# Router logits of seven blocks: VectorE products with a running sum in place of TensorE transposes and matmuls

## Chip, cores and metric

One core of one Trainium2 chip. The metric is the device time of one execution in microseconds (us); lower is better. Engines are called by the names of the profile: PE is TensorE (PEld its weight loads), DVE is VectorE, ACT is ScalarE, POOL is GpSimd, SP is SyncE, which here only issues DMAs.

## The reference, cut to what matters

```python
# attention over keys and values pooled by 8, 8 heads of 64, 8 batches of 576 rows
x = attention(q, k, v)                      # 4608 rows of 512
h = x @ w_in                                # 4608 x 2048
g = where(h >= 1, h, where(h <= -1, 0, (h + 1)**2 / 4))
x = g @ w_out                               # 4608 x 512, called Y below
logits = x @ w_gate                         # 4608 x 8
e = argmax(logits); p = softmax(logits)[e]
out = p * (relu(x @ w1[e]) @ w2[e])         # each row with the weights of its own expert
```

The change concerns the line `logits = x @ w_gate` alone.

## The kernel before

The 4608 rows are 36 tiles of 128 rows, grouped in ten blocks: block 0 has 3 tiles, blocks 1 to 7 have 4, block 8 has 3 and block 9 has 2. A block is one pass over `w_in` and `w_out` in 16 steps, called m = 0 to 15 here. Step m of block j issues, in this order: `f1` for two steps ahead (12 matmuls with the hidden rows as output), slot 2m, `f2` for step m (3 matmuls for each tile, summed in one PSUM bank per tile over the 16 steps), slot 2m+1. Each engine runs its own queue in the order in which the code emits it, so this order is the order on PE, DVE, ACT, POOL and SP.

Behind each `f1` stands a chain over two engines: DVE cuts to -1..1 (line 489, here the clip), ACT squares (490), DVE takes the maximum (494), ACT rounds to the high part (495), DVE writes the low part (501, here the last link). `f1` of step m uses the PSUM bank of step m-2, so it can only start when the last link of step m-2 is done; `f2` of a step needs the same link of its own step. The maximum is emitted in slot 2m and the last link in slot 2m+1.

A slot also takes units of the attention of the next block from a list (`units`): transposes and small matmuls on PE, softmax work on DVE, ACT and POOL, and the pooling of keys and values on DVE (line 212). Units and routing share two PSUM banks in turn. Last, a slot takes steps of the routing of the block before from a queue, `todo`: one step in even slots and two in odd ones, and two in every slot of blocks 8 and 9. Empty steps stand in the queue for spacing.

`route_steps(j)` fills that queue for block j at the start of block j+1. For each tile, `turn` transposes the rows of Y on PE (4 transposes) and ACT copies the result to `YT`. `logits_t` multiplies with the gate weights `WGT` (4 matmuls of 512 columns, seen as 8 in the trace), ACT copies to `LT`. `logits` transposes back (one per tile) and DVE adds up into `LG` (line 550). Then `s1` picks the expert (DVE lines 563 to 569), `s2` finds the position of each row (DVE lines 579 to 590) and SP stores Y to `yrow_d` (line 591), and `s3` has POOL scatter the row numbers with one indirect DMA per tile (line 598). `YT` and `LT` lie in the tile `WG`, which is otherwise free in these blocks. SP issues the loads of the first expert's weights (line 667) after the store of block 7's rows.

Of the kernel before, what the change touches and what calls it, by code (L numbers as in the profile page):

```python
# [8 lines left out]
F32 = mybir.dt.float32  # L9
# [3 lines left out]
ACTF = mybir.ActivationFunctionType  # L13
ALU = mybir.AluOpType
# [9 lines left out]
def attention_ffn_routed_experts_kernel(  # L24
# [12 lines left out]
    nc = tc.nc  # L37
    B, H, S, D = q.shape
    NT, DM = out.shape
    DFF = w_in.shape[1]  # L40
    NE, _, EF = w1.shape
    NTILE = NT // 128
    SP_ = S // 8
    KD = DM // 128
# [12 lines left out]
    blocks, t = [], 0  # L57
# [3 lines left out]
    NB = len(blocks)  # L61
# [5 lines left out]
    dram = ctx.enter_context(tc.tile_pool(name="dram", bufs=1, space=bass.MemoryType.DRAM))  # L67

    wo_d = dram.tile([KF, 128, 2, DM], F32R, name="wo_d")
    yrow_d = dram.tile([NT + 128, ROW], F32, name="yrow_d")  # L70
    perm_d = dram.tile([NE * CAP, 1], I32, name="perm_d")

# [13 lines left out]
    FX = sb.tile([128, 4112], F32, name="FX")  # L86
    Y = sb.tile([128, 4, ROW], F32, name="Y")
    WG = sb.tile([128, NE, DM], F32, name="WG")
    YO = [WG[:, 4 + i] for i in range(4)]
    YT = WG[:, 0:4]  # L90
    LT = WG[:, 4]
    WGT = sb.tile([128, KD, NE], F32, name="WGT")
# [4 lines left out]
    def fx(o, n):  # L97
# [11 lines left out]
          for a in [YF[:, 0:1024], YF[:, 1024:2048], at(5312, 1024)]  # L109
          + [WG.rearrange("p e d -> p (e d)")[:, 1024 * i:1024 * (i + 1)] for i in range(3)]]  # L110
    JK = at(6848, 512)
# [17 lines left out]
    ident = sb.tile([128, 128], F32, name="ident")  # L129
# [31 lines left out]
    LG = sb.tile([128, 4, NE], F32, name="LG")  # L161
# [59 lines left out]
    def bank():  # L221
        banks.rotate(-1)
        return banks[-1]
# [29 lines left out]
    SCH = at(6848, 576)  # L253
    WGF = WG.rearrange("p e d -> p (e d)")[0:SP_]
    PTX = [WOF[2][0:SP_], WOF[3][0:SP_]] + [WGF[:, 3072 + 512 * i:3584 + 512 * i] for i in range(2)]
# [191 lines left out]
    n = FIRST  # L447
# [74 lines left out]
    def route_steps(j, bk):  # L522
        t0, n = blocks[j]
# [3 lines left out]
        V = nc.vector  # L527
        st = []

        def turn(t):  # L530
            pb = bk()
            for c in range(KD):
                nc.tensor.transpose(pb[:, c * 128:(c + 1) * 128], Y[:, t, c * 128:(c + 1) * 128],
                                    ident)
            nc.scalar.activation(out=YT[:, t], in_=pb, func=ACTF.Copy)

        def logits_t():

            pb = bk()
            for c in range(KD):  # L540
                nc.tensor.matmul(pb[32 * c:32 * c + NE, 0:n * 128], WGT[:, c],
                                 YT[:, 0:n, c * 128:(c + 1) * 128], start=True, stop=True)
            nc.scalar.activation(out=LT[:, 0:n * 128], in_=pb[:, 0:n * 128], func=ACTF.Copy)
# [7 lines left out]
                out=lg, in_=pb[:, 0:n * 128].rearrange("p (t c x) -> p t x c", c=KD, x=32)[:, :, 0:NE],  # L551
                axis=AX.X, op=ALU.add)

        wait = 2 if j < NB - 2 else 1
        for t in range(n):
            st.append(lambda t=t: turn(t))
            st.extend([lambda: None] * wait)
        for f in (logits_t, logits):
            st.append(f)
            st.extend([lambda: None] * wait)  # L560

        def s1():
            V.tensor_reduce(out=mx, in_=lg, axis=AX.X, op=ALU.max)
# [365 lines left out]
    with tc.manual_schedule():  # L929

        pre = [WG[0:SP_, i] for i in range(8)]
        raw0 = pre + RAW + [FX[0:SP_, 512 * i:512 * (i + 1)] for i in range(1, 5)] + [JK[0:SP_]]
# [100 lines left out]
        for g, (j, m) in enumerate(steps):  # L1033
            if m == 0:
                if j:
                    evict_y(j - 1)
                    todo.extend(route_steps(j - 1, bank))
                    banks.clear()
                    banks.extend(ps[6:8])
                lim = blocks[j + 1][0] + blocks[j + 1][1] - 1 if j + 1 < NB else -1  # L1040
                cnt = 0
                for i, u in enumerate(units):
                    if u[0] <= lim:
                        cnt = i + 1
                state["units"], state["done"] = cnt, 0
                if j == 1:

                    nc.vector.memset(JK, 0.0)
                    nc.vector.memset(Y[:, :, DM:ROW], 0.0)
                    nc.scalar.dma_start(out=yrow_d[NT:NT + 128, 0:DM], in_=JK)  # L1050
                    nc.scalar.dma_start(out=yrow_d[NT:NT + 128, DM:ROW], in_=Y[:, 3, DM:ROW])
            if g + AHEAD < len(steps):
                f1(*steps[g + AHEAD])
            else:
                f1e(0, g + AHEAD - len(steps))
            slot(j, 2 * m)
            f2(j, m)
            if (j, m) == (0, KF - 2):
                more_consts()
                nc.vector.memset(CB[:, 0], 0.0)  # L1060

                pr = at(6848, NE * CAP // 128).bitcast(I32)
                nc.gpsimd.iota(pr, pattern=[[1, NE * CAP // 128]], base=0,
                               channel_multiplier=NE * CAP // 128)
                nc.vector.tensor_scalar(pr, pr, 127, None, op0=ALU.bitwise_and)
                nc.vector.tensor_scalar(pr, pr, float(NT), None, op0=ALU.add)
                nc.sync.dma_start(out=perm_d.rearrange("(p r) o -> p (r o)", p=128), in_=pr)
            slot(j, 2 * m + 1)
        evict_y(NB - 1)
        todo.extend(route_steps(NB - 1, bank))  # L1070
# [166 lines left out]
```

## Time and profile before

| what | us |
|---|---|
| median of 3 runs (1577.69 to 1592.39) | 1578.44 |
| profiled execution | 1580.64 |
| its span, first to last instruction | 1578.9 |
| PE busy | 1457.9 (92%) |
| DVE busy | 793.5 (50%) |
| ACT busy | 489.0 (31%) |
| POOL busy | 214.0 (14%) |

The blocks can be told by line 519, the copies of Y at a block's end: block 1 begins at 191.9 us, block 2 at 299.9, 3 at 408.6, 4 at 517.2, 5 at 625.7, 6 at 734.1, 7 at 843.3, 8 at 944.9, 9 at 1030.2; the expert part begins at 1105.0. Matmuls overlap in the records: one of 512 columns is shown with 0.39 us and the next starts 0.23 us later, so PE's cost is read from start to start. The same holds for DVE: an instruction that waits for nothing starts before the record of the one ahead has ended.

### The profile page before, as it was taken

What the parts mean: (1) busy time and instruction counts of PE and PEld (TensorE: products, weight loads), DVE (VectorE), ACT (ScalarE), POOL (GpSimd) and SP (SyncE); (2) the same over time, 40 slices, a digit from 0 to 9 for tenths busy, and PEclk for the clock granted to TensorE, in tenths of its full rate; (3) what the DMA queues carried; (4) which work ended last, traced back from release to release, by engine and by line L of the source; (5) the groups of instructions that cost most, each with busy time, mean ns of one, the idle gap of its engine ahead of it and who ended that gap; (6) DMA issues with size and microseconds to landing.
All of it is one profiled execution on the core that took longest, in us unless ns stands there. A gap on an engine that the chain in (4) does not pass through costs nothing. (4 is left out here: it accounts for less than half of the span.)

```text
span 1578.9 us, 19781 instructions
## 1 busy us (share of the span) xinstructions
PE 1457.9 (92%) x7415; PEld 1185.9 (75%) x7415; DVE 793.5 (50%) x1547; ACT 489.0 (31%) x900; POOL 214.0 (14%) x216
## 2 busy tenths in 40 slices
PE   5677799999999999999999999886699999999797
PEld 4566677778777777777778788775588888888685
DVE  6898756646555654665654445343232222212425
ACT  5344332333332333332333333232111111111334
POOL 4222101001001001001010010002321111111211
PEclk8899999999999999999999999997899999999999
DMA  8566436427629456465475384974141101110403
GB/s 226 161 207 198 134 118 122 127 90 126 131 90 142 122 109 97 130 128 95 132 105 97 100 89 137 201 155 86 41 168 54 54 28 40 44 51 28 159 28 140
DMA packets 102550, 177.28 MB, mean 112 GB/s; under 512 B 46594, under 2 KB 54933, under 8 KB 102432
## 3 DMA queue, kind: packets, MB, share of 16 engines
q10 hardware_dynamic: 21552, 75.79, 24.0%
q1 hardware_dynamic: 73392, 79.93, 17.8%
q0 software_dynamic: 7488, 20.07, 4.3%
q8 instruction: 64, 1.05, 0.3%
q14 instruction: 54, 0.44, 0.1%
HBM read 171.05 MB, written 28.29 MB: 126 GB/s over the span
## 5 line engine op out<-in xcount | busy, mean ns | idle before, releaser
L482 PE MATMUL ps<-XT,W 128*128 128x512 f32 (+2 forms) x640 | 252.1, 394 | 9.1 <-DVE FG L501 8.4
L510 PE MATMUL ps<-WO,FG 128*128 128x512 f32 x576 | 241.6, 419 | 20.2 <-ACT WO L438 10.7
L483 PE MATMUL ps<-XT,W 128*128 128x512 f32 (+2 forms) x640 | 239.9, 375 | 3.0 <-DVE XT L344 3.0
L484 PE MATMUL ps<-XT,W 128*128 128x512 f32 (+2 forms) x640 | 240.0, 375 | 1.5 <-POOL W L226 1.5
L511 PE MATMUL ps<-WO,FG 128*128 128x512 f32 x576 | 230.7, 400 | 3.9 <-POOL WO L226 2.7
L490 ACT ACTIVATE FX<-FX,half 128x512 f32<-128x512 f32 (+2 forms) x152 | 104.0, 684 | 413.7 <-DVE FX L489 406.7
L512 PE MATMUL ps<-WO,FG 128*128 128x512 f32 x576 | 229.9, 399 | 0.0
L489 DVE TENSOR_SCALAR FX<-ps 128x512 f32<-128x512 f32 (+2 forms) x152 | 96.6, 635 | 181.8 <-PE ps L484 181.6
L820 DVE SCALAR_TENSOR_TENSOR FG<-ps,FG 128x512 fp32r<-128x512 f32 (+1 forms) x64 | 43.2, 675 | 220.7 <-ACT FG L819 220.7
L510 PEld LDWEIGHTS ps<-WO,FG 128*128 128x128 f32 x576 | 110.5, 192 | 51.2 <-issue 13.5
L482 PEld LDWEIGHTS ps<-XT,W 128*128 128x128 f32 x640 | 123.5, 193 | 32.0 <-DVE FG L501 9.7
L484 PEld LDWEIGHTS ps<-XT,W 128*128 128x128 f32 x640 | 123.0, 192 | 21.7 <-POOL W L226 2.4
L483 PEld LDWEIGHTS ps<-XT,W 128*128 128x128 f32 x640 | 123.7, 193 | 19.9 <-DVE XT L344 3.9
L495 ACT ACTIVATE FG<-ps 128x512 fp32r<-128x512 f32 (+2 forms) x160 | 88.9, 555 | 148.1 <-DVE ps L494 136.7
L511 PEld LDWEIGHTS ps<-WO,FG 128*128 128x128 f32 x576 | 111.0, 193 | 26.4 <-POOL WO L226 4.1
L512 PEld LDWEIGHTS ps<-WO,FG 128*128 128x128 f32 x576 | 110.6, 192 | 25.1
L494 DVE TENSOR_TENSOR ps<-FX,ps 128x512 f32<-128x512 f32 (+2 forms) x152 | 97.4, 640 | 56.6 <-ACT FX L490 56.6
L501 DVE TENSOR_TENSOR FG<-ps,FG 128x512 fp32r<-128x512 f32 (+2 forms) x160 | 100.8, 630 | 39.7 <-ACT FG L495 39.7
L819 ACT ACTIVATE FG<-ps 128x512 fp32r<-128x512 f32 (+1 forms) x64 | 37.5, 585 | 266.0 <-PE ps L816 265.5
L317 POOL TENSOR_TENSOR AT<-AT,ssm 128x576 f32<-128x576 f32 x36 | 42.6, 1186 | 488.6 <-DVE ssm L310 422.3
L814 PE MATMUL ps<-XT,W 128*128 128x512 f32 (+1 forms) x256 | 99.0, 387 | 0.0
L815 PE MATMUL ps<-XT,W 128*128 128x512 f32 (+1 forms) x256 | 98.6, 385 | 0.0
(215 smaller groups left out, 2281.1 us busy)
## 6 DMA issues: line engine op xcount, KB each, us to landing
WO<-wo_d ACTq DMA_DIRECT2D x144, 512.0 KB
AT<-in_moe_w_dram SPq DMA_DIRECT2D x10, 2048.0 KB
AT<-in_moe_w_dram SPq DMA_DIRECT2D x14, 1024.0 KB
AT<-in_v_dram SPq DMA_DIRECT2D x60, 144.0 KB
AT<-in_q_dram SPq DMA_DIRECT2D x32, 256.0 KB
wo_d<-WO SPq DMA_DIRECT2D x16, 512.0 KB
AT<-in_k_dram SPq DMA_DIRECT2D x56, 144.0 KB
yrow_d<-Y SPq DMA_DIRECT2D x7, 1032.0 KB
```

The source lines that it names most:

```text
L482: nc.tensor.matmul(o, wi(m, 0, c), xh, start=(c == 0), stop=False)
L483: nc.tensor.matmul(o, wi(m, 0, c), xl, start=False, stop=False)
L484: nc.tensor.matmul(o, wi(m, 1, c), xh, start=False, stop=(c == KD - 1))
L489: nc.vector.tensor_scalar(r, o, -1.0, 1.0, op0=ALU.max, op1=ALU.min)
L490: nc.scalar.activation(out=r, in_=r, func=ACTF.Square, scale=0.5, bias=half)
L494: nc.vector.tensor_tensor(out=o, in0=r, in1=o, op=ALU.max)
L501: nc.vector.tensor_tensor(out=gl, in0=o, in1=r32(gh), op=ALU.subtract)
L510: nc.tensor.matmul(o, gh, WO[:, g % 4, 0], start=(m == 0), stop=False)
L511: nc.tensor.matmul(o, gh, WO[:, g % 4, 1], start=False, stop=False)
L512: nc.tensor.matmul(o, gl, WO[:, g % 4, 0], start=False, stop=(m == KF - 1))
L814: nc.tensor.matmul(o, e1(0)[:, c, ms], xh, start=(c == 0), stop=False)
L815: nc.tensor.matmul(o, e1(0)[:, c, ms], xl, start=False, stop=False)
```

## The change

For blocks 1 to 7 the steps `turn`, `logits_t` and `logits` are gone. In their place stand 32 instructions `logit(t, e)` on DVE, one for each tile and expert: 512 products of a row of Y and a gate column, with their sum in `LG`. They come in pairs, one pair to a step of the queue. For blocks 1 to 6 an empty step follows most pairs, so that a tile takes 7 steps of the queue; for block 7 there is none, and a slot of block 8 takes two pairs. The products themselves go to the scratch `JK`, the same one each time. The gate columns must lie along the row on every partition: at the start of block 1, PE transposes `WGT` (4 transposes), ACT copies, SP stores 16 KB to DRAM (`wg_d`), and at step 13 of block 1 ACT's queue issues a DMA that loads it to all 128 partitions of `WG` (2 MB). Blocks 0, 8 and 9 keep the way of before.

```diff
+        def logit(t, e):
+            V.scalar_tensor_tensor(out=JK, in0=Y[:, t, 0:DM], scalar=1.0, in1=WG[:, e],
+                                   op0=ALU.mult, op1=ALU.mult, accum_out=LG[:, t, e:e + 1])
...
-        wait = 2 if j < NB - 2 else 1
-        for t in range(n):
-            st.append(lambda t=t: turn(t))
-            st.extend([lambda: None] * wait)
-        for f in (logits_t, logits):
-            st.append(f)
-            st.extend([lambda: None] * wait)
+        if 0 < j < NB - 2:
+            for i in range(0, n * NE, 2):
+                st.append(lambda i=i: [logit(*divmod(x, NE)) for x in (i, i + 1)])
+                st.extend([lambda: None] * (j < NB - 3 and i % 8 > 0))
+        else:
+            wait = 2 if j < NB - 2 else 1
+            for t in range(n):
+                st.append(lambda t=t: turn(t))
+                st.extend([lambda: None] * wait)
+            for f in (logits_t, logits):
+                st.append(f)
+                st.extend([lambda: None] * wait)
...
+                    pb = bank()
+                    for c in range(KD):
+                        nc.tensor.transpose(pb[0:NE, c * 128:(c + 1) * 128], WGT[:, c], ident)
+                    nc.scalar.activation(out=LT[0:NE], in_=pb[0:NE], func=ACTF.Copy)
+                    nc.sync.dma_start(out=wg_d, in_=LT[0:NE])
...
+            if (j, m) == (1, 13):
+                nc.scalar.dma_start(out=WG, in_=wg_d.unsqueeze(0).to_broadcast([128, NE, DM]))
```

## Rows read from the trace of the kernel before

**Rows 1.** Windows by block (1, 3): length, busy us of engines, PEclk, DMA share, GB/s.

```profile
191.90:299.90 108.00, 105.52 (x553) 83.85 (x552) 70.26 (x128) 36.50 (x68) 7.76 (x7) 1.00 0.54 128
...
408.60:517.20 108.60, 107.72 (x565) 85.89 (x564) 65.42 (x122) 36.93 (x68) 8.49 (x8) 1.00 0.58 122
```

**Rows 2.** Timeline of PE in block 3: start, us, instruction, idle before and releaser.

```profile
413.06 0.63 PE L533 MATMUL ps<-ident,Y 128*128 128x128 f32 x4 [0.88 <-DVE AT L300]
...
420.22 0.66 PE L533 MATMUL ps<-ident,Y 128*128 128x128 f32 x4
420.63 0.47 PE L510 MATMUL ps<-WO,FG 128*128 128x512 f32 x1
...
441.06 1.04 PE L541 MATMUL ps<-WG,WGT 128*8 128x512 f32 x8
442.04 0.50 PE L510 MATMUL ps<-WO,FG 128*128 128x512 f32 x1
```

**Rows 3.** Windows of steps m=0 to 8 (blocks 3, 2, 5, 7), then m=0 to 3 of block 8.

```profile
411.30:475.95 64.65, 63.77 (x348) 50.54 (x347) 39.52 (x83) 23.01 (x42) 4.46 (x4) 1.00 0.36 115
...
302.58:367.61 65.03, 64.16 (x360) 50.30 (x359) 33.16 (x75) 22.41 (x40) 4.46 (x4) 1.00 0.29 90
...
628.35:693.15 64.80, 63.92 (x348) 50.73 (x347) 45.87 (x90) 23.22 (x42) 4.45 (x4) 1.00 0.42 129
...
845.96:906.82 60.86, 60.86 (x336) 48.69 (x335) 28.14 (x65) 20.39 (x36) 3.30 (x3) 1.00 0.28 93
947.36:969.40 22.04, 22.04 (x134) 18.94 (x133) 11.39 (x33) 8.49 (x16) 1.14 (x1) 1.00 0.36 129
```

**Rows 4.** DVE instructions with two SBUF inputs: a line's durations (ns), a group's mean.

```profile
L427 DVE SCALAR_TENSOR_TENSOR FX<-AT,FX x5: 672/682/685, 38.3 to 149.7; 128x512 int32<-128x512 int32 x5
...
L891 DVE TENSOR_TENSOR W<-AT,W 128x1024 fp32r<-128x1024 f32 x14 | 16.5, 1222 | 11.8 <-ACT W L889 6.1 <-ACT FX L863 5.7
```

**Rows 5.** Timeline of DVE in block 3.

```profile
409.37 1.28 DVE L517 COPY Y<-ps 128x512 f32<-128x512 f32 x2
...
472.57 0.18 DVE L581 TENSOR_TENSOR G<-ps,CB 128x32 f32<-128x32 f32 x1
472.79 0.17 DVE L583 COPY CB<-CB 128x8 f32<-128x8 f32 x1
472.87 0.19 DVE L584 TENSOR_TENSOR G<-G,ebase 128x32 f32<-128x32 f32 x1
```

**Rows 6.** Timeline of ACT in the first tile's softmax, with a sum as second output.

```profile
23.67 0.32 ACT L296 ACTIVATE AT<-ps,smx 128x72 f32<-128x72 f32 x1 [2.91 <-PE ps L283]
23.89 0.19 ACT L296 ACTIVATION_READ_ACCUMULATOR AT<-ps,smx 128x1 f32 x1
23.98 0.31 ACT L296 ACTIVATE AT<-ps,smx 128x72 f32<-128x72 f32 x1
```

**Rows 7.** Timeline of POOL and DVE in block 0.

```profile
45.31 1.74 POOL L226 TENSOR_TENSOR W<-FX,W 128x512 fp32r<-128x512 f32 x1 [3.63 <-ACT W L438]
...
45.93 1.66 DVE L427 SCALAR_TENSOR_TENSOR FX<-WG,FX 128x512 int32<-128x512 int32 x1
```

**Rows 8.** Waits of DVE from 411.30 to 475.95 us: total, times, longest.

```profile
DVE XT L344 <- ACT XT L343: 5.2, 5, 1.1
...
DVE ps L494 <- ACT FX L490: 2.4, 3, 0.8
```

**Rows 9.** Timeline of block 3: the last link of a step, and the `f1` that waits for it.

```profile
418.90 0.68 DVE L501 TENSOR_TENSOR FG<-ps,FG 128x512 fp32r<-128x512 f32 x1
...
423.82 0.48 PE L482 MATMUL ps<-XT,W 128*128 128x512 f32 x1
```

**Rows 10.** Block 8: SP's loads of expert weights, then PE's longest wait (timelines).

```profile
984.57 2.78 SPq L667 DMA_DIRECT2D AT<-in_moe_w_dram  x4
...
1007.60 0.76 PE L510 MATMUL ps<-WO,FG 128*128 128x512 f32 x1 [5.15 <-DMA WO<-wo_d]
```

**Rows 11.** The page's DMA queues, ACT's: packets, MB, share of 16 engines.

```profile
q10 hardware_dynamic: 21552, 75.79, 24.0%
```

More of the change, by code (lines that the diff above doesn't have):

```diff
@@ L69, in attention_ffn_routed_experts_kernel @@
     wo_d = dram.tile([KF, 128, 2, DM], F32R, name="wo_d")
+    wg_d = dram.tile([NE, DM], F32, name="wg_d")
     yrow_d = dram.tile([NT + 128, ROW], F32, name="yrow_d")
```

## The prediction

> **What bounds the kernel now.** I read the windows cut at the block boundaries first. In block 3 PE is busy for 107.7 of 108.6 us at the full granted clock and DVE for 65.4 [rows 1]. So PE sets the length of these blocks, and what is taken off PE shortens them, as long as the other queues keep up. Block 1 shows where that ends: there DVE has 70.3 us of work in 108.0, and PE already loses 2.5 us [rows 1]. Then I read PE's timeline for the price of the routing steps, the windows of the steps m = 0 to 8, in which the new DVE work is to stand, and last DVE's waits and the slack between its last link and the `f1` that needs it.
>
> **What goes off PE.** A turn takes 0.41 us from its start to the next matmul's, `logits_t` 0.98 [rows 2], and I take 0.41 again for the four transposes back: 4 x 0.41 + 0.98 + 0.41 = 3.0 us a block. The first turn also waits 0.88 us for a bank that DVE still reads [rows 2]; the same wait stands once in each of blocks 2 to 6. That makes 3.9 us in these five and 3.0 in blocks 7 and 8, 25.5 us in all. This is the ceiling of the gain. ACT's five copies a block go too; ACT is idle most of the time, so I price them at nothing.
>
> **What one logit costs DVE.** No row shows a DVE product with a running sum, so I bound it. The main instruction has two SBUF inputs of 512 four-byte elements, as line 427 has: 0.68 us [rows 4]. Two copies that wait for nothing take 1.28 us together, so the second starts 0.60 us after the first [rows 5]. On ACT the sum comes out by an instruction of its own, which starts 0.22 us after a main one of 0.32 us and holds the queue for 0.09 us more [rows 6]. Lower end: 0.60 for the main one and 0.08 for a small one that waits for nothing (L583 to L584 [rows 5]), 0.68 us. Upper end: both run to their end, with 0.04 us each before the next starts: 0.68 + 0.04 + 0.17 + 0.04 = 0.93 us. I take 0.80: the read overlaps as on ACT (0.60 + 0.17), but the next product overwrites the same `JK`, and L583, which overwrites what L581 reads, starts 0.22 us after it, which is its 0.18 and 0.04 more [rows 5]. That adds 0.04. So 32 logits are 25.6 us a block, between 21.8 and 29.8.
>
> The Trainium skill ("VectorE: DVE Perf Modes", section "Two Vector instructions with no wait between them") also has an accumulator output as two instructions; no row here shows that for DVE, and if the read were free the sum would be that of the lower end.
>
> **Whether DVE keeps up.** The steps of `todo` put the 32 logits into m = 0 to 8 (28 steps of the queue at 1.5 a slot), and s1 and s2, which stood there, move behind. These are some 20 small instructions with the sum of line 550, at 0.2 us each (0.18 and 0.04 [rows 5]): 4.0 us less. In its order DVE also has idle time that no later work can fill: it waits for ACT within its own chains, 5.2 + 2.4 = 7.6 us in these nine steps [rows 8]. So for m = 0 to 8 of block 3 DVE needs 39.5 - 4.0 + 25.6 + 7.6 = 68.7 us, and PE, 3.9 us lighter, 64.65 - 3.9 = 60.8 [rows 3]. DVE becomes the bound, by 7.9 us. Part of it is slack: the last link ends at 419.58 and the `f1` that needs it starts at 423.82 [rows 9], 4.2 us later. PE then waits 7.9 - 4.2 = 3.7 us, and of the 3.9 us 0.2 are left. Block 4 has the same work. Block 2, from its own row: 33.2 - 4.0 + 25.6 + 7.6 = 62.4 against 61.1, inside the slack: gain 3.9. Block 7: 28.1 - 4.0 + 25.6 + 7.6 = 57.3 against 57.9: gain 3.0 [rows 3]. Blocks 5 and 6 have more pooling in these steps [rows 3]: 45.9 - 4.0 + 25.6 = 67.5 if the pooling fills the waits, 75.1 if not, against 60.9. After the slack PE waits 2.4 to 10.0 us; I take the middle, 6.2, a loss of 2.3 each. Blocks 2 to 7 together: 3.9 + 0.2 + 0.2 - 2.3 - 2.3 + 3.0, a gain of 2.7 us. The logits stand behind the maximum and the last link in DVE's queue, so it is the next clip, softmax pieces and the low part of attention rows that come late, and through them `f1` and the units two banks on.
>
> **Block 8** is where it hurts. Two pairs stand in each slot, so all 32 logits lie in m = 0 to 3, which last 22.0 us and have 11.4 us of DVE work [rows 3]. DVE needs 11.4 + 25.6 and for four steps 0.85 us of waits each (7.6 / 9), 40.4 us; PE 22.0 - 3.0 = 19.0. After 4.2 us of slack PE waits some 17 us, a loss of 14. Some comes back: later in the block PE waits 5.15 us for a load of `w_out` that shares the DMA engines with the expert weights [rows 10]. These loads stand behind Y's store on SP and so behind s2, which is now one slot earlier in order but late by DVE's lag. If PE arrives later than the loads do, the wait shrinks, by 0 to 5.15; I take 2.5. Loss of block 8: 11.5 us.
>
> **The rest.** The prelude of block 1 is one turn more on PE, 0.5 us. The 2 MB to all partitions: ACT's queue moves 75.79 MB in 24% of the span of 16 engines [rows 11], 379 us, so 2.1 MB are some 10.5 us; it is issued near 288 us (step 13 of block 1) and first needed after the maximum of block 2's first step, near 305. The cover is 17 us, and I price it at nothing; if it lands late, the first logit holds the whole DVE queue, at most 10 us once. `w_out` loads queue behind it on ACT's ring, but each is issued three steps, some 20 us, before its use. On SP one store of 16 KB more is nothing; SP's loads of queries and keys pass the later s2 in order, so nothing of theirs waits for it longer. Y's store moves from m = 8 to m = 11 and needs to land by the block's end, some 25 us later: hidden. POOL: a two-input DVE instruction took 1.66 us beside a POOL instruction of 1.74 [rows 7], 1.0 more than alone. POOL's softmax product runs 4 times a block; if two in five meet a logit in the steps that DVE bounds, that is 2 us.
>
> **Sum.** -2.7 + 11.5 + 0.5 + 2.0 = +11.3 us. Against the profiled execution, 1580.6, that is 1591.9; the median of the runs lies 2.2 us lower, so 1589.7, and I say 1589. A measurement of this kernel can tell about 1% (16 us), so this is no change that can be told, leaning to slower.
>
> **Rivals.** (1) DVE has room and the ceiling is paid out: 65.4 us of its 108.6 are used, 19 or 25 more still fit on average. Then the time is 1578.4 - 25.5 + 0.5 = 1553. It holds if the logits fall into DVE's waits for PE rather than beside work. Against it: the order is fixed, the logits fill nine steps of sixteen, and block 1 loses time at 70 us. 14%. (1b) The cheap end, 0.68 us: 3.8 us less a block. Blocks 3 and 4 then gain 3.9 each, blocks 5 and 6 1.5, block 8 loses 7.7: -17.7 + 7.7 + 0.5 + 1 = -8.5, 1570; within 1%. 13%.
> (2) Slower: the read of the sum does not overlap, 0.93 us a logit. It decides from about 0.83 on, where the sum passes 1%. Then blocks 3 to 6 and 8 lose 4.2 us more each and block 2 leaves its slack by 1.3: 11.3 + 21.0 + 5.2 = 37.5 at most, 1612 to 1616. 22%.
> (3) The product with a sum runs at half rate. Line 427 has two four-byte SBUF inputs and is not halved [rows 4], but it writes no sum. At half rate the main one costs what 1024 elements do, 1.22 us [rows 4], with 0.13 for the read 1.35; that is 0.55 x 32 = 17.6 us a block more in five blocks, 14.7 in block 2 and 12.8 in block 7: +127, 1705. 8%.
> The Trainium skill ("Vector Engine (DVE) Microarchitecture Reference", section "Points that are easy to get wrong") says so: this shape with two SBUF sources that are not bf16 halves throughput, as no read port is left for the accumulator. By that rule the time is that of rival 3; the trace speaks neither for nor against it where a sum is written.
>
> **How the numbers follow.** My forecast (0.72 to 0.88 us a logit) has 43%, and three quarters of it lie within 1%, the rest above. With 1b: same 0.44; slower 0.40 (rivals 2, 3 and that rest); faster 0.16 (rival 1 and a little of 1b). The range of 8 in 10 goes from near rival 1 to beyond rival 2, 1556 to 1624; rival 3 is left out above and half of rival 1 below.
>
> **What would show it.** DVE's logit rows give the cost from start to start. In the windows, m = 0 to 8 of blocks 3 to 6 should be as long as before, with PE idle before `f1` and released by line 501; blocks 2 and 7 shorter by 3 to 4 us; the first four steps of block 8 longer by 10 to 14 us. If PE is never held by line 501, my slack is too small and rival 1 is right. If blocks 3 to 6 grow by over 5 us, the cost per logit is the wrong term. A wait of DVE for the load of the gate columns near 305 us would be a miss of another kind.

## The result

The changed kernel takes 1596.07 us (median of 20 runs, 1589.92 to 1602.71); the kernel before, in 20 runs beside it, 1582.98. The ratio is 1.0081 with a 95% interval of 1.0065 to 1.0096: slower by 0.8%, inside the 1% that the prediction called no change. The forecast was 1589. The profiled execution of the changed kernel was its longest, 1602.71 (span 1601.0), 6.6 us above the median.

First the same cut as in [rows 1], one window per block from the first Y eviction to the next (DVE's here; there it was ACT's, 0.7 us earlier, and the lengths agree within 0.1 us); blocks 1, 2, 3, 7 and 8 of the changed kernel (columns as there):

```profile
192.83:309.10 116.27, 109.54 (x552) 86.91 (x551) 70.15 (x130) 37.17 (x69) 7.77 (x7) 0.96 0.55 137
309.10:413.80 104.70, 104.70 (x556) 83.40 (x555) 81.08 (x180) 33.20 (x60) 7.31 (x6) 1.00 0.42 113
413.80:524.45 110.65, 106.38 (x536) 84.79 (x535) 86.92 (x186) 33.78 (x62) 9.30 (x8) 0.98 0.51 117
...
856.57:954.65 98.08, 98.08 (x509) 80.09 (x508) 68.20 (x161) 30.31 (x53) 7.60 (x7) 1.00 0.54 100
954.65:1052.91 98.26, 78.82 (x397) 67.52 (x397) 56.92 (x157) 22.20 (x45) 8.23 (x8) 0.93 0.66 143
```

Blocks 2 and 7 keep PE busy for their whole length, with nothing lost. Block 3 has DVE busy for 86.9 us where [rows 1] has 65.4, and PE, which should have been 4 us lighter, loses 4.3 us and some of its granted clock. Block 8 loses 19.4 us of PE.

These are the lengths of all blocks (from eviction to eviction, each worked out from the start times of DVE's first eviction), for the kernel before, the change and the experiments below:

```
kernel               b1     b2     b3     b4     b5     b6     b7    b8    b9   b3-6
before             108.1  108.7  108.6  108.5  108.4  109.2  101.4  85.1  74.5  434.7
the change         116.3  104.7  110.7  110.5  110.9  110.8   98.1  98.3  74.7  442.8
its second profile 117.8  104.7  110.7  109.6  110.0  112.1   98.1  99.1  76.4  442.4
e1 prelude only    109.5  108.7  108.3  108.8  108.5  109.2  101.4  83.9  75.0  434.7
e2 block 7 PE      110.4  104.7  110.6  109.6  110.1  112.8   98.1  83.3  76.1  443.2
e3 two blocks      109.5  104.7  108.3  108.8  108.4  109.2   98.1  85.7  76.1  434.7
e4 even singles    109.9  104.8  107.7  108.1  105.3  108.5   98.0  85.0  75.2  429.6
e5 even pairs      109.5  104.8  108.2  107.5  107.0  107.9   98.0  85.1  77.5  430.6
e6 b7 singles      110.4  104.8  107.7  106.5  105.3  106.7   98.0  81.8  81.0  426.2
e7 load only       115.9  109.6  111.0  112.7  111.8  113.7  101.5  86.4  73.6  449.2
e8 saving only     109.4  104.7  104.1  104.6  104.2  104.9   98.1  85.9  76.8  417.7
e9 no POOL product 109.5  104.8  105.2  105.8  106.0  105.9   98.0  92.3  77.4  422.8
e11 even slots     109.1  107.1  107.6  106.5  109.1  108.8   98.1  84.4  74.5  431.9
e12 set apart      111.5  106.5  109.0  104.3  113.4  110.4   98.1  83.0  81.4  437.1
```

Block j's logits are formed in block j + 1, so the change acts on blocks 2 to 8; block 1 has only the prelude. In the two profiled executions of the change it is blocks 2 and 7 that gain (4.0 and 3.3 us), blocks 3 to 6 that lose (8.1 and 7.7 us together), block 8 that loses 13 to 14, and block 1 that is 8 to 10 us longer. Each row is one profiled execution. Where the same instructions run, blocks 3 to 6 repeat well: 442.8 and 442.4 us in the two profiles of the change, 434.7 three times on PE's way (before, e1, e3).

Now the price of a logit. The timeline of DVE in block 3 of the changed kernel shows one pair:

```profile
419.22 0.68 DVE L496 TENSOR_TENSOR ps<-FX,ps 128x512 f32<-128x512 f32 x1
419.82 0.68 DVE L540 SCALAR_TENSOR_TENSOR AT<-Y,WG 128x512 f32<-128x512 f32 x1
420.43 0.08 DVE L540 DVE_READ_ACCUMULATOR AT<-Y,WG 128x1 f32 x1
420.54 0.69 DVE L540 SCALAR_TENSOR_TENSOR AT<-Y,WG 128x512 f32<-128x512 f32 x1
421.15 0.08 DVE L540 DVE_READ_ACCUMULATOR AT<-Y,WG 128x1 f32 x1
421.15 0.46 DVE L292 TENSOR_REDUCE smx<-ps 128x4 f32<-128x288 f32 x1
```

The next piece of work starts together with the second read, 421.15 - 419.82 = 1.33 us after the pair began: 0.665 us a logit and 21.3 us a block. The two do not cost the same: the second logit begins 0.72 us after the first, the work behind the second 0.61 us after it. The main instruction takes what line 427 takes in [rows 4]. The groups by line of the same kernel (count | busy us, mean ns | idle before):

```profile
L540 DVE SCALAR_TENSOR_TENSOR AT<-Y,WG 128x512 f32<-128x512 f32 x224 | 166.8, 745 | 4.4
...
L540 DVE DVE_READ_ACCUMULATOR AT<-Y,WG 128x1 f32 x224 | 18.2, 81 | 0.0
```

The mean of the main one is 745 ns, not 680: some of the 224 take more than twice as long. One of them, in block 3, shows the whole chain of the loss. First the timeline of DVE, POOL, ACT and the two waits of PE, in order of time, then the windows over the same place:

```profile
454.15 0.20 DVE L312 RECIPROCAL ssm<-ssm 128x8 f32<-128x8 f32 x1
454.27 0.64 DVE L540 SCALAR_TENSOR_TENSOR AT<-Y,WG 128x512 f32<-128x512 f32 x1
454.52 1.40 POOL L319 TENSOR_TENSOR AT<-AT,ssm 128x576 f32<-128x576 f32 x1 [26.43 <-DVE ssm L312]
...
454.95 1.52 DVE L540 SCALAR_TENSOR_TENSOR AT<-Y,WG 128x512 f32<-128x512 f32 x1
...
456.40 0.68 DVE L491 TENSOR_SCALAR FX<-ps 128x512 f32<-128x512 f32 x1
457.12 0.72 ACT L492 ACTIVATE FX<-FX,half 128x512 f32<-128x512 f32 x1 [3.99 <-DVE FX L491]
457.74 0.36 ACT L345 ACTIVATE XT<-ps 128x256 fp32r<-128x256 f32 x1
458.14 0.42 DVE L346 SCALAR_TENSOR_TENSOR XT<-ps,XT 128x256 fp32r<-128x256 f32 x1 [1.06 <-ACT XT L345]
...
458.62 0.66 PE L274 MATMUL ps<-ident,AT 128*128 128x128 f32 x4 [1.98 <-DVE XT L346]
...
462.37 0.69 DVE L491 TENSOR_SCALAR FX<-ps 128x512 f32<-128x512 f32 x1
463.09 0.72 ACT L492 ACTIVATE FX<-FX,half 128x512 f32<-128x512 f32 x1 [2.73 <-DVE FX L491]
463.71 0.58 ACT L276 ACTIVATE AT<-ps 128x512 f32<-128x512 f32 x1
...
464.35 1.02 PE L285 MATMUL ps<-AT 128*128 128x144 f32 x4 [1.72 <-ACT AT L276]
```

```profile
454.00:458.00 4.00, 2.64 (x12) 1.84 (x10) 3.01 (x7) 0.88 (x2) 1.40 (x1) 1.00 0.00 0
458.00:462.00 4.00, 3.38 (x18) 2.60 (x18) 3.79 (x10) 1.21 (x3) 0.00 (x0) 1.00 0.21 59
462.00:466.00 4.00, 2.28 (x15) 1.87 (x15) 2.27 (x6) 2.08 (x4) 0.00 (x0) 0.84 0.50 159
466.00:470.00 4.00, 4.00 (x17) 3.18 (x16) 3.13 (x8) 0.00 (x0) 0.00 (x0) 0.74 0.29 110
```

DVE finishes the reciprocal of a softmax (L312), and POOL's product with it starts at once. The two logits of the same slot stand directly behind the reciprocal on DVE, so the second one meets POOL and takes 1.52 us. The clip (L491) is behind it. ACT's square (L492) waits 3.99 us for that clip, and ACT's copy of an attention unit (L345), next in ACT's queue, comes late with it; its low part (L346) frees the bank for which PE waits 1.98 us. One step later four logits stand between the maximum and the next clip. That clip is late again, the square waits 2.73 us, and behind it ACT's copy of the queries (L276) is late, which PE multiplies in L285: this wait, 1.72 us, is for data and not for a bank. So the delay goes from DVE through ACT's queue to PE. After that the granted clock shows 0.84 and 0.74 of full speed in two windows. In 454 to 470 PE idles for 3.7 us, and the clock costs, as an estimate from these windows, 0.16 x 4 + 0.26 x 4 = 1.7 more: 5.4 of the 6.5 us by which this block is longer than block 3 without any logits (104.1, e8). The starts of `f1` say the same: measured from the block's start, the seventh `f1` of the block begins 3.2 us sooner than in the kernel before, the ninth 2.4 us later.

PE's waits over blocks 3 to 6 of the changed kernel (us in total, times, longest):

```profile
PE ps L274 <- DVE XT L346: 4.5, 4, 2.0
PE ps L285 <- ACT AT L276: 3.9, 4, 1.7
PE ps L484 <- DVE FG L503: 3.1, 4, 1.1
PE ps L285 <- DVE AT L302: 1.9, 2, 0.9
PE ps L245 <- DVE XT L346: 1.6, 2, 0.8
```

Only 3.1 us of them are `f1` held by the last link (line 501 before, L503 here). Most belong to the attention units: banks that come free late (8.0 us, the rows with L346 and L302) and the queries that ACT copies late (3.9 us, L276). In all four of the latter ACT's copy stands directly behind a square that waited for a clip. Block 8 shows another picture; DVE's timeline in its first slots, and PE's waits in all of it:

```profile
960.70 0.69 DVE L540 SCALAR_TENSOR_TENSOR AT<-Y,WG 128x512 f32<-128x512 f32 x1
961.32 0.08 DVE L540 DVE_READ_ACCUMULATOR AT<-Y,WG 128x1 f32 x1
961.32 0.15 DVE L638 TENSOR_REDUCE MX<-CB 128x1 f32<-128x8 f32 x1
...
963.18 0.15 DVE L651 CAST RWM<-POSF 128x1 int32<-128x1 f32 x1
963.25 0.55 DVE L503 TENSOR_TENSOR FG<-ps,FG 128x384 fp32r<-128x384 f32 x1
963.72 0.68 DVE L540 SCALAR_TENSOR_TENSOR AT<-Y,WG 128x512 f32<-128x512 f32 x1
```

```profile
PE ps L484 <- DVE FG L503: 9.5, 4, 5.0
PE ps L512 <- DMA WO<-wo_d: 9.4, 3, 5.1
```

Four logits stand between the parts of each link (two pairs to a slot, two slots to a step). In the first slot the eleven small instructions that pick the first expert (L638 to L651) come on top. PE waits four times for the link, 9.5 us, and then still waits for `w_out`.

### The profile page after: what moved, and what is told of

It reads as the page before. It is cut to its first block, busy times and chain, and to the rows that moved or that the text cites. A ratio compares the mean times of both kernels' runs of the same rounds, so it can differ in the third digit from the quotient of the medians.

```text
span 1601.0 us, 19800 instructions
## 1 busy us (share of the span) xinstructions
PE 1453.6 (91%) x7223; PEld 1182.0 (74%) x7223; DVE 945.7 (59%) x1988; ACT 468.1 (29%) x866; POOL 219.2 (14%) x216
## 3 DMA queue, kind: packets, MB, share of 16 engines
q10 hardware_dynamic: 21696, 77.88, 22.5%
## 5 line engine op out<-in xcount | busy, mean ns | idle before, releaser
L484 PE MATMUL ps<-XT,W 128*128 128x512 f32 (+2 forms) x640 | 256.2, 400 | 25.0 <-DVE FG L503 24.0
L485 PE MATMUL ps<-XT,W 128*128 128x512 f32 (+2 forms) x640 | 243.4, 380 | 3.0 <-DVE XT L346 3.0
L486 PE MATMUL ps<-XT,W 128*128 128x512 f32 (+2 forms) x640 | 243.4, 380 | 1.5 <-POOL W L228 1.5
L492 ACT ACTIVATE FX<-FX,half 128x512 f32<-128x512 f32 (+2 forms) x152 | 104.0, 684 | 469.9 <-DVE FX L491 462.1
L540 DVE SCALAR_TENSOR_TENSOR AT<-Y,WG 128x512 f32<-128x512 f32 x224 | 166.8, 745 | 4.4
L484 PEld LDWEIGHTS ps<-XT,W 128*128 128x128 f32 x640 | 125.9, 197 | 50.3 <-DVE FG L503 29.0
L491 DVE TENSOR_SCALAR FX<-ps 128x512 f32<-128x512 f32 (+2 forms) x152 | 96.6, 635 | 89.6 <-PE ps L486 89.3
L512 PEld LDWEIGHTS ps<-WO,FG 128*128 128x128 f32 x576 | 111.4, 193 | 49.2 <-issue 11.3
L486 PEld LDWEIGHTS ps<-XT,W 128*128 128x128 f32 x640 | 125.6, 196 | 22.1 <-POOL W L228 2.4
L485 PEld LDWEIGHTS ps<-XT,W 128*128 128x128 f32 x640 | 126.2, 197 | 20.2 <-DVE XT L346 3.9
L503 DVE TENSOR_TENSOR FG<-ps,FG 128x512 fp32r<-128x512 f32 (+2 forms) x160 | 100.9, 630 | 34.1 <-ACT FG L497 34.1
L319 POOL TENSOR_TENSOR AT<-AT,ssm 128x576 f32<-128x576 f32 x36 | 46.1, 1283 | 504.5 <-DVE ssm L312 412.2
L825 PE MATMUL ps<-XT,W 128*128 128x512 f32 (+1 forms) x256 | 99.0, 387 | 0.0
```

Source lines behind the costliest of these rows:

```text
L484: nc.tensor.matmul(o, wi(m, 0, c), xh, start=(c == 0), stop=False)
L485: nc.tensor.matmul(o, wi(m, 0, c), xl, start=False, stop=False)
L486: nc.tensor.matmul(o, wi(m, 1, c), xh, start=False, stop=(c == KD - 1))
L491: nc.vector.tensor_scalar(r, o, -1.0, 1.0, op0=ALU.max, op1=ALU.min)
L492: nc.scalar.activation(out=r, in_=r, func=ACTF.Square, scale=0.5, bias=half)
L503: nc.vector.tensor_tensor(out=gl, in0=o, in1=r32(gh), op=ALU.subtract)
```

## The experiments

All are edits of the changed kernel. Where the total is given as a ratio, it is to the kernel before, run beside it on the same chip.

**e1: the prelude alone.**

```
-        if 0 < j < NB - 2:
+        if False:
```

> All blocks keep PE's way; only the prelude of block 1 (transposes, copy, 16 KB store) and the 2 MB load to all partitions stay, and nobody uses them. Theory A, the prelude itself costs: block 1, which was 8.3 us longer in the changed kernel (116.3 against 108.0), stays longer by 3 us (PE's wait of 2.6 us for the bank that ACT's copy holds, and 0.4 us of transposes) up to 8; the other blocks are as before; the time is 3 to 8 us above before. Theory B, block 1 was longer in that one profile by chance (late loads of V): block 1 within 1 us of 108.0, the time within 1 us of before.

Measured: 1585.54 us (12 runs), ratio 0.9994, interval 0.9974 to 1.0015. Blocks 2 to 7 are as before within 0.3 us; block 1 is 1.4 us longer, where PE waits 2.6 us for the bank that ACT copies in the prelude (L1066). Neither theory fits block 1 (A had 3 us or more, B at most 1); the total is B's. So the prelude and the 2 MB load do not explain the time of the change.

**e2: block 7 back on PE's way.**

```
-        if 0 < j < NB - 2:
+        if 0 < j < NB - 3:
```

> Block 7 goes back to PE's way; blocks 1 to 6 stay as changed. Theory A, the 32 logits packed into four steps make block 8 long: block 8 is back at 85.3 us (98.4 in the changed kernel), the time falls by 11 to 13 us to that of before, within 3 us. Theory B, block 8 is long because its loads of w_out and of expert weights collide whatever DVE does: block 8 stays at 92 or more and less than half of the 13 us comes back.

Measured: 1585.38 us (12 runs), ratio 1.0006, 0.9984 to 1.0028. Block 8 falls from 98.3 to 83.3 us; blocks 3 to 6 stay as in the change (443.2 and 442.8). Against the kernel before, run beside each, 13.1 us more have become 0.3: block 8 alone accounts for the loss of the whole, and blocks 2 to 7 are worth nothing together.

**e3: VectorE only for blocks 1 and 6.**

```
-        if 0 < j < NB - 2:
+        if j in (1, 6):
```

> Logits on DVE for blocks 1 and 6 alone, so that only blocks 2 and 7 carry them, where DVE has the least other work in the steps that hold the logits. Theory A, PE sets the length where DVE has room and the logits cost nothing there: block 2 at 104.7 and block 7 at 98.4 as in the changed kernel, blocks 3 to 6 back at 108.5, block 8 at 85.3; the time is 7.3 us under before plus what block 1's prelude costs, so between -4 and +1 us against before. Theory B, blocks 2 and 7 were shorter only because the blocks around them left work behind or took it: they come out within 1 us of 108.7 and 101.6.

Measured: 1601.13 us (6 runs), ratio 1.0085, 1.0052 to 1.0118. PE's way in blocks 2 to 5 writes its transposes over the gate weights in `WG`, so block 6 is routed by other numbers; the expert part differs, and the total can't be compared. The block lengths can: blocks 2 and 7 are 104.7 and 98.1, as in the change, and blocks 3 to 6 together are 434.7, as before. What the change does in a block stays in that block.

**e4: even singles,** blocks 1 to 6, block 7 on PE's way: one logit to a step without empty steps, so at most two in a slot instead of four.

```
-        if 0 < j < NB - 2:
-            for i in range(0, n * NE, 2):
-                st.append(lambda i=i: [logit(*divmod(x, NE)) for x in (i, i + 1)])
-                st.extend([lambda: None] * (j < NB - 3 and i % 8 > 0))
+        if 0 < j < NB - 3:
+            for i in range(n * NE):
+                st.append(lambda i=i: logit(*divmod(i, NE)))
```

> As the run with block 7 on PE's way, but the logits of blocks 1 to 6 stand one by one, one to each step of the queue and no empty steps: 3 to a step of the block instead of mostly 4, over 10.7 steps instead of 9. Theory A, the packing sets what blocks 3 to 6 lose, since DVE's whole work (87 of 110.8 us in block 3) would fit: they fall from 110.3-110.9 to 106-108 us, the time is 10 to 16 us under the run with block 7 on PE's way. Theory B, DVE's order as a whole is what binds, however the logits are spaced: blocks 3 to 6 stay within 1 us of 110.6, the time within 4 us of that run.

Measured: 1568.69 us (6 runs), ratio 0.9898, 0.9859 to 0.9936: 1.0% faster than before, the fastest kernel here that leaves nothing out. Blocks 3 to 6 take 429.6 us instead of 443.2 with the same logits in the same blocks (e2). The packing of the steps cost these 13.6 us, not the amount of work; nor is it POOL, since 25 of the 192 logits overlap its product here and 26 in e2 (by more than 0.15 us). The total is 16.7 us below e2's, a little more than theory A's 16.

**e5: even pairs.** Each pair followed by an empty step, so 32 steps as in e4; block 7 on PE's way.

```
-                st.extend([lambda: None] * (j < NB - 3 and i % 8 > 0))
+                st.extend([lambda: None] * 1)
```

> Blocks 1 to 6 on VectorE as pairs, each pair followed by an empty step (32 steps, never more than two logits to a slot), block 7 on PE's way. Against the run with single logits, which has the same 32 steps, only the pairing differs; against the run with the change's own packing and block 7 on PE's way, only the density. Theory A (density: where two pairs fall into one slot, VectorE is 2.7 us behind and the link of the next chunk comes late): blocks 3 to 6 together 428 to 433 us, as with singles (429.6), and 1566 to 1573 us in all. Rival P (a pair is itself too long, since it holds back a link by 1.33 us whatever stands around it): blocks 3 to 6 together 439 us or more, nearer the 443.1 of the change's packing, and 1578 to 1587 us in all.

Measured: 1575.24 us (6 runs), ratio 0.9924, 0.9895 to 0.9954. Blocks 3 to 6: 430.6 us, as with singles. The total is 2 us above what theory A gave, while the lengths of blocks 3 to 6 are as it gave them; a pair in itself costs nothing. Density in a slot decides.

**e6: block 7 on VectorE too, all as even singles.**

```
-        if 0 < j < NB - 2:
-            for i in range(0, n * NE, 2):
-                st.append(lambda i=i: [logit(*divmod(x, NE)) for x in (i, i + 1)])
-                st.extend([lambda: None] * (j < NB - 3 and i % 8 > 0))
+        if 0 < j < NB - 2:
+            for i in range(n * NE):
+                st.append(lambda i=i: logit(*divmod(i, NE)))
```

> All of blocks 1 to 7 on VectorE, single logits with no empty step: in block 8, where a slot takes two steps, at most two logits to a slot instead of four. Against the run with even singles for blocks 1 to 6, only block 7's way differs. Theory A (density): block 8 takes at most 87 us (98.4 in the change, 85.0 with block 7 on PE's way), and the time is 1563 to 1573 us. Rival B (amount: block 8 has no room for 21 us more of VectorE, as its chunks are short and it takes 14 us of other work): block 8 takes 92 us or more, and the time is 1575 us or more.

Measured: 1575.30 us (7 runs), ratio 0.9928, 0.9897 to 0.9959. Windows of blocks 8 and 9:

```profile
933.16:1014.94 81.78, 73.40 (x391) 63.38 (x391) 54.81 (x157) 21.81 (x44) 6.49 (x7) 0.98 0.69 142
1014.94:1095.92 80.98, 59.97 (x331) 51.18 (x330) 27.87 (x76) 24.75 (x47) 12.44 (x10) 0.83 0.71 141
```

Block 8 takes 81.8 us with all 32 logits on DVE, 16.5 less than in the change and 3.2 less than in e4. So there is room for them; for block 8 amount is refuted and density shown. The total did not follow, it is 2.3 us above theory A's range: block 9 is 5.8 us longer than in e4, with 8.6 us of PE waiting for `w_out` instead of 3.3 (but 12.2 for gathered rows instead of 16.2) and a granted clock of 0.83 instead of 0.86. Blocks 8 and 9 together take 162.8 us, 160.2 in e4 and 173.0 in the change. Whether the longer block 9 follows from block 8 being shorter or from its later routing was not tried.

**e7: the load without the saving.** PE's way stays; the products run beside it in the change's own steps, with rows 5 to 7 of the gate weights, into a scratch.

```
...
+            more = []
+            for i in range(0, n * NE, 2):
+                more.append(lambda i=i: [extra(*divmod(x, NE)) for x in (i, i + 1)])
+                more.extend([lambda: None] * (i % 8 > 0))
+            st += [lambda: None] * (len(more) - len(st))
+            st = [lambda f=f, h=h: (f(), h()) for f, h in zip(st, more)]
...
```

> PE's way kept for all blocks, and beside it, in the same steps as in the change, VectorE forms the 32 products of a block with rows of the gate weights (only rows 5 to 7, which PE's way does not overwrite) and writes the sums to a place that nobody reads: the load without the saving, in blocks 2 to 7 of the trace (blocks 1 to 6's logits). Theory A (the saving is about 4 us everywhere and the packed load takes back the difference): blocks 2 and 7 stay within 1 us of 108.7 and 101.4; blocks 3 to 6 become 4 to 7 us longer each (112.5 to 116), 1602 to 1616 us in all. Rival C (the loss appears only because a faster PE comes to the banks earlier; with PE's way kept there is room): blocks 3 to 6 less than 2.5 us longer each, 1585 to 1597 us in all.

Measured: 1600.78 us (5 runs), ratio 1.0084, 1.0055 to 1.0113. Blocks 2 and 7 are 0.8 and 0.1 us longer than before; blocks 3 to 6 2.5 to 4.5, 14.5 us together. That lies between the two theories.

**e8: the saving without the load.** No logits for blocks 1 to 6; the empty steps stay.

```
...
-                st.append(lambda i=i: [logit(*divmod(x, NE)) for x in (i, i + 1)])
+                st.append(lambda: None)
```

> The logits of blocks 1 to 6 are not computed at all (those blocks are routed by block 0's logits, so what follows the last block differs and the total says little); the empty steps stay where the products were, and block 7 is on PE's way. Read are the lengths of blocks 2 to 7: the saving without the load. Theory A: each of blocks 2 to 7 is 3.3 to 4.3 us shorter than before, blocks 3 to 6 together 418 to 421 us (434.7 before). Rival D (something other than VectorE's products takes the saving back, such as ScalarE's banks): blocks 3 to 6 are shorter by less than 2.5 us each, 425 us or more together.

Measured: 1546.60 us, a total that says little; the lengths say much. Windows of blocks 2 and 3:

```profile
300.39:405.05 104.66, 104.66 (x556) 83.41 (x555) 58.79 (x116) 33.88 (x60) 6.57 (x6) 1.00 0.42 114
405.05:509.16 104.11, 104.11 (x536) 83.56 (x535) 65.28 (x123) 34.42 (x62) 8.50 (x8) 1.00 0.59 125
```

PE is busy for all of each block. Blocks 2 to 7 are 4.1, 4.5, 3.9, 4.3, 4.3 and 3.3 us shorter than before, 24.3 in all: this is the ceiling, and theory A's 418 to 421 for blocks 3 to 6 came out as 417.7. Against it the change loses 442.8 - 417.7 = 25.1 us in blocks 3 to 6 (16.3 of it are PE's waits there, five of whose eight rows stand above; the other 8.8 are near what the clock accounts for, 0.98 over the 332 us of blocks 3, 4 and 6: 6.6). The same load beside PE's slower way cost 14.5 (e7): the load and the saving do not add. A freed PE comes to each bank sooner, which may be why; no run tries that by itself.

**e9: e4 without POOL's product.** The softmax of every row tile after the third is not divided by its row sums.

```
                 if t >= HEAD:
-                    later.append(norm)
+                    pass
```

> The run with even singles (blocks 1 to 6 on VectorE, 429.6 us for blocks 3 to 6, 1568.7 us in all), with the division of the softmax left out on GpSimd for every row tile after the first three (the 1.28 us product beside which a logit took up to 1.5 instead of 0.68 us; attention is then not divided by its row sums, so the numbers differ, the amount of other work does not). Against it only the collision of VectorE and GpSimd is gone. Theory A (density and the links alone): blocks 3 to 6 stay at 427 to 431 us. Rival G (the collisions, about 12 us of VectorE's time in the run, are what still makes the links late): blocks 3 to 6 fall to 418 to 423 us, near the 417.7 of the run without logits, and the whole by 7 to 12 us, to 1557 to 1562 us.

Measured: blocks 3 to 6 take 422.8 us instead of 429.6. The total, 1622.88 us, belongs to other routing and can't be compared. The mean of the logit's main instruction is 682 ns here and 741 in e4 (192 of them):

```profile
L540 DVE SCALAR_TENSOR_TENSOR AT<-Y,WG 128x512 f32<-128x512 f32 x192 | 130.9, 682 | 2.1
```

So the slow logits are those beside POOL, and they make 6.8 of the 11.9 us that e4 still loses against e8. POOL's product alone costs nothing there: in e8 it runs without logits, and PE waits for nothing in blocks 3 to 6. The remaining 5.1 us are there without POOL; PE waits 3.9 us in them, 3.7 of it for the queries that ACT copies late (L276), each time behind a square that waited for its clip.

**e10: the change once more.** No edit; a second profile.

> The changed kernel as it is, for a second profile. Open is block 1: 116.3 us in the first profile, 108.1 before, 109.4 to 110.4 in five kernels that run the same instructions up to its end. Theory A (an accident of that execution, which was the longest of its 20): block 1 takes 109 to 111 us, blocks 3 to 6 together 442 to 444 us, block 8 97 to 100 us, and the profiled time is 1592 to 1599 us. Rival B (it belongs to the change): block 1 takes 115 us or more again.

Measured: 1597.86 us (4 runs), ratio 1.0076, 1.0054 to 1.0097; the profiled execution took 1605.27. Block 1 takes 117.8 us, long again, so it is no accident of one execution: theory A fell, and rival B's 115 us or more came. The timeline of the first profile shows the place: SP's issue of four loads of V, DVE's wait for one of them, the last link, and `f1`; then the windows over it.

```profile
274.31 13.50 SPq L208 DMA_DIRECT2D AT<-in_v_dram  x4
...
286.47 1.01 DVE L214 TENSOR_REDUCE VS<-AT 72x64 f32<-72x512 f32 x1 [4.43 <-DMA AT<-in_v_dram]
287.40 0.68 DVE L503 TENSOR_TENSOR FG<-ps,FG 128x512 fp32r<-128x512 f32 x1
...
288.13 0.79 PE L484 MATMUL ps<-XT,W 128*128 128x512 f32 x1 [3.89 <-DVE FG L503]
```

```profile
284.00:288.00 4.00, 0.24 (x3) 0.00 (x0) 1.53 (x3) 0.00 (x0) 0.00 (x0) 0.90 0.89 269
288.00:292.00 4.00, 3.87 (x9) 3.10 (x10) 2.92 (x5) 2.51 (x5) 0.00 (x0) 0.50 0.61 153
292.00:296.00 4.00, 4.00 (x19) 2.72 (x19) 1.29 (x3) 1.00 (x2) 0.00 (x0) 0.75 0.32 124
```

The four loads hold SP's queue for 13.50 us, in the second profile for 14.87, and in the kernel before for 9.85. The link waits behind the pooling of V on DVE, PE waits 3.89 us and then runs at the lower clock level. Seven other kernels here (e1 to e6, e11) run the same instructions up to the end of block 1 and take 109.1 to 110.4 us in it; in e2 the four loads took 10.47. What makes them slower in the change, and in e7, stays open. The profiled executions of the change are 6.6 and 7.4 us above their medians, so the median run may have little of it; that is argued, not shown.

**e11: two logits in the even slot, one in the odd one,** otherwise e4.

```
-            for i in range(n * NE):
-                st.append(lambda i=i: logit(*divmod(i, NE)))
+            for i in range(0, n * NE, 3):
+                st.append(lambda i=i: [logit(*divmod(x, NE)) for x in (i, i + 1)])
+                st.append(lambda i=i: [logit(*divmod(x, NE)) for x in (i + 2,) if x < n * NE])
+                st.append(lambda: None)
```

> The run with even singles, but with two logits in the slot between the first and the second product of a chunk and one in the slot after it, instead of one and two (pair, single, empty step; still three logits to a chunk). Theory A (what counts is how many logits lie in one slot, not in which): blocks 3 to 6 within 3 us of 429.6 and 1566 to 1573 us in all. Rival S (a logit in the second slot lies directly before the clip of the next chunk, in the first it lies before nothing urgent): blocks 3 to 6 at most 424 us and 1560 to 1564 us in all; or the other way, 435 us or more.

Measured: 1573.75 us (12 runs), ratio 0.9947, 0.9924 to 0.9971; blocks 3 to 6 431.9 us, within theory A's 3 us. The total is 0.8 us above its range. Which of a step's two slots holds the dense one matters little; block 2 is 2.4 us longer than in e4.

**e12: logits kept out of the slots with POOL's product,** otherwise e4.

```
...
-                if todo:
+                if todo and not (shared and hasattr(todo[0], "hot")):
                     todo.popleft()()
+            shared.clear()
```

`shared` is filled when a softmax's reciprocal is queued, `hot` marks a logit.

> The run with even singles, but a slot in which the row sums of a softmax were just inverted (GpSimd's product starts right then) takes no logit; the logits wait for the next slot. Nothing is left out, 32 logits a block as before. Theory G (the logits beside GpSimd's product make the links late): no logit above 1 us in blocks 3 to 6, these blocks together 421 to 426 us (429.6 with even singles, 422.8 without GpSimd's product), 1560 to 1566 us in all. Rival H (the instruction that now meets GpSimd's product is a clip or a maximum of the link itself, which is worse): the clip or maximum shows 1.2 us and more there, and blocks 3 to 6 stay at 429 us or more, 1568 us or more in all.

Measured: 1581.64 us (12 runs), ratio 0.9968, 0.9951 to 0.9984, blocks 3 to 6 437.1 us. The design was flawed: the logits put off made the queue of steps longer than a block, so the routing of one block ran into the next and took part of its numbers from the next block's Y, and in block 4 PE waited 4.3 us for Y's eviction behind the late store; neither the total nor the lengths answer the question. Less those 4.3 us the four blocks take 432.8 us, no less than in e4, so the run gives theory G no support either. What it does show is the group of the logits:

```profile
L542 DVE SCALAR_TENSOR_TENSOR AT<-Y,WG 128x512 f32<-128x512 f32 x192 | 133.3, 694 | 2.2
```

694 ns against 741: kept out of that slot, only three of the 192 logits still meet POOL's product (25 do in e4). Rival H's slow clip did not come: ten clips of 128x512 overlap POOL's product now, and none takes over 0.69 us. Whether the 6.8 us can be had in a kernel that keeps its routing inside the block is open.

## Why the prediction was right, and where its steps were not

The class and nearly the size came out: forecast 1589, measured 1596.07. Of the 7 us between them 4.5 lie in the kernel before: the forecast started from the median of three runs, 1578.44, and 20 runs give 1582.98. As a rise, 11.3 us were forecast and 13.1 measured. That it came so near is in part luck: two terms were wrong in opposite directions.

**The ceiling** was right. 3.9 us in blocks 2 to 6 and 3.0 in block 7 were worked out from [rows 2], 22.5 us together; e8 measures 24.3.

**The price of a logit** was mis-sized. 0.80 us was taken, from the copy of [rows 5], ACT's read and a hazard on `JK`; measured are 0.665, just below the lower end. The read starts while the main one ends (420.43 to 420.50), and other work starts together with it, 0.61 us after the main one: it costs such work nothing. Only a logit directly behind another starts later, 0.11 us after the read and 0.04 after the main one's end. That is the 0.04 that the prediction added for `JK`, but whether `JK` causes it was not tried, and the second logit of each pair is free of it. Rivals 2 and 3 fell with that. (Two slips in the prediction change nothing here: a read that costs nothing makes 0.60 us a logit, less than the lower end to which it is put; and the 5.2 us in rival 2's sum are 3.9 too many, for block 2 leaves its slack by 1.3 alone.) The rule of the Trainium skill ("Vector Engine (DVE) Microarchitecture Reference", section "Points that are easy to get wrong") that this shape halves throughput with two SBUF sources that are not bf16 does not hold here: 0.68 us with a sum, 0.68 us without [rows 4], and 0.68 us for the last link, which has one SBUF input [rows 9]. The Trainium skill ("VectorE: DVE Perf Modes", section "Two Vector instructions with no wait between them") has the sum as an instruction of its own, and the trace agrees: 0.08 us.

**Whether DVE keeps up** is the step that failed. By its own sum, 0.665 us gives 39.5 - 4.0 + 21.3 + 7.6 = 64.4 us against PE's 60.8, and the 4.2 us of slack [rows 9] cover that: blocks 3 and 4 should have gained 3.9 each, as rival 1b has it, and the whole should have come to some 1570. They lost 2.1 and 2.0. A sum over nine steps let idle time of one step pay for the load of another, and took one link's slack for the slack of all. In the trace the loss lies in single slots, where four logits or a POOL product come together. It reaches PE mostly through the attention units, which the prediction named ("two banks on") but did not price: the late clip holds ACT's square, the square holds the copies behind it, and PE waits for a bank or for the queries. The sign that the prediction gave, PE released by line 501, accounts for 3.1 of 16.3 us. e4 shows that the same 32 logits, at most two to a slot, cost 13.6 us less.

**POOL** was mis-sized: 2 us were put down for the whole kernel; e9 shows 6.8 us in blocks 3 to 6 even with even singles. Chance ("two in five") was the wrong model: the logits stand right behind the reciprocal that starts POOL. In the place shown POOL's product ends at 455.92 and the logit that began at 454.95 at 456.47, 0.55 us later. It is the same every time: all sixteen logits of the change that took over 1 us, ten of them in blocks 3 to 6, end 0.54 to 0.56 us after a product of POOL's, and none of the 194 that overlap no such product took over 0.69. This agrees with a rule of the Trainium skill ("SBUF — State Buffer", section "Who interferes with whom"): a VectorE instruction with two SBUF inputs and a GpSimd one that reads SBUF exclude each other, and the later one is blocked until the first is done. Clip, maximum and link have at most one SBUF input, so by that rule the change brought onto VectorE just the kind that meets POOL. The trace of the kernel before agrees: 14 clips, one maximum and three links of 128x512 overlap POOL's product there by more than 0.15 us, and none takes over 0.69 us.

**Blocks 2 and 7** came out as said, gains of 3.9 and 3.0 against 4.0 and 3.3 measured. **Blocks 5 and 6**, forecast at a loss of 2.3 each, lost 2.4 and 1.6, the right size for the wrong reason, since the cheaper logit would have turned that into a gain.

**Block 8** was right in place and reason: the link L503 holds `f1`, as foreseen. The size, a loss of 11.5 forecast and 13.2 measured (15.0 between the change and e2), is in part luck. PE waits 9.5 us for the link where some 17 were put down. The part that should have come back did not: the waits for `w_out` are 9.4 us, 7.0 before, and the block's granted clock is 0.93, 0.96 before. The first four steps are 5.6 us longer, not 10 to 14, and the next two 4.9. e6 shows that it is the density and not the amount of work.

**The rest.** The prelude's 0.5 us are 1.4 in e1, and nothing that the time shows. The 2 MB load at nothing was right: the first logit, at 315.12 us, waits for no DMA. The long block 1 of the change was not foreseen, and its cause is open.

The sum, term by term against the profile: blocks 2 to 7 +0.8 (forecast -2.7), block 8 +13.2 (+11.5), block 9 +0.2, the prelude with +1.4 from e1: +15.6, where the medians differ by 13.1.

## What to carry to other kernels

Work moved to an engine that is 60% busy is priced by the slot, not by the block: ask what stands behind it in that engine's queue, which banks those instructions free, what waits for them in the queues of other engines, and how many come together; spreading the same work, and leaving the short block to PE, turned +0.8% into -1.0%. Measure the saving and the load apart (no work at all, then both ways at once), since they need not add: here -17.0 and +14.5 us made +8.1. And look at what the instruction just ahead sets off on another engine, for the new work will run beside that every time and not by chance.

## What the runs showed that was not expected

A DVE product that also sums costs no more than one that doesn't, 0.68 us for 128x512 four-byte elements. The read of the sum, 0.08 us, delays other work by nothing, and a second such product starts 0.11 us after it. Beside POOL's product of 128x576 the same instruction took 1.52 us. PE can pay twice for a wait: after the 3.89 us of block 1 the granted clock was 0.50 in one window of 4 us, the lower level (1.2 of 2.4 GHz), and 0.75 in the next, a mean of both levels; by 0.50 x 4 + 0.25 x 4 that adds, as an estimate, 3 us to the wait; after the 1.98 and 1.72 us in block 3 it was 0.84 and 0.74. It does not pay each time: in block 5 of the change PE waits 5.3 us in all, 1.64 us at most at a time, and the mean clock of the block is 1.00.
